# A retention layer and a token/channel mixer on one core: the state recurrence as one scan, the first token mixing inside the channel sums, wide q rows, and a scheduler that simulates its DMA queues

## The chip, the core and the metric

The kernel runs on one core of a Trainium2 chip. Times are device microseconds (us) of that core. The engines are called TensorE (PE, matmul; PEld is its weight load), VectorE (DVE), ScalarE (ACT), GpSimd (POOL) and SyncE (SP). Each takes its own instructions in the order in which the program holds them; semaphores make one wait for another. Sixteen DMA engines move the data, fed by queues: q1 is fed by SP, q0 by POOL, q10 by ACT.

## The reference

The first stage is a retention recurrence over q, k and v of shape (4 batches, 8 heads, 768 tokens, 64). The second is a mixer: over the tokens, then over the channels, each with a relu and a residual sum.

```
gamma = 1 - 2 ** (-5 - arange(8));  scale = 1 / sqrt(64)
for t in range(768):
    state = gamma * state + outer(k[t], v[t])          # 64 x 64 for each batch and head
    y[t]  = scale * q[t] @ state
x  = y as (4, 768, 512)                                # heads side by side
u  = x + (relu(x.T @ w_tok1) @ w_tok2).T               # w_tok1 768 x 256, w_tok2 256 x 768
out = u + relu(u @ w_ch1) @ w_ch2                      # w_ch1 512 x 1536, w_ch2 1536 x 512
```

Everything is float32 at the outside; the matmuls take float16.

## The kernel before, in words

The tokens of a batch are split into six chunks of 128, the heads into four pairs of two (128 channels). The unit of the front is one pair p of one batch b, written (b,p); the unit of the back is half a batch, 384 tokens.

The front of a pair (`front`, L338) does this:
- `load` (L313) has brought k and q as float32 through SP's queue (tiles kf and qf, L325 and L322) and v as float16 through POOL's (L333). k is scaled by gamma to the power of minus the place in the chunk (L376 on ACT, L378 on DVE), q is only cast (L384, L386).
- k and q are turned so that the channels lie on the partitions: in batches 0 and 1 by TensorE transposes (L412) and a copy out of PSUM (L423), in batches 2 and 3 by transposing DMAs on SP's queue (L403).
- ST (L439): ten matmuls give the sum of k times v of each of the first five chunks, for both heads. A DVE copy (L448) and four instructions (L451) carry the state from chunk to chunk: U[c] = U[c-1] * gamma^128 + ST[c]. Two scalings (L462 or L464) write it as float16 into r16.
- QK (L482): twelve matmuls give the k-by-q products within the chunks; four DVE products with a triangular mask (L490) give am. Y (L504, L507) adds state times q and am times v. X (L520, L524) scales Y by the decay of the token and is kept as float32; L537 casts it (x16).
- T1 (L548, twelve matmuls) and a relu (L556) give h1 of the token mixing. In batches 1 to 3 T2 (L599, two groups of six) applies w_tok2, L607 adds it to X, L615 casts u, and u is turned into uT by transposes (L636, L642) or by a DMA (L626). In batch 0 uT comes straight from TensorE: G (L570, L573) sums w_tok2 times h1 and the transposed x in PSUM, L580 copies it out. There T2 and L607 are done as well, later, because X has to hold u for the last sum.

The back of a batch (`back`, L651) does, for each half: C1 (L668), 12 groups of four 384-wide matmuls with a relu each (L682), then C2 (L695), three groups of twelve 512-wide matmuls, each followed by a sum with X on DVE (L703) and a store through ACT's queue (L709).

The order of the work is not written by hand. Each step is an `Op` with the engines it may run on, costs, the ops it needs, and the buffers (`Slot`) that it takes. `arrange` (L123) places them one after the other by estimated start and priority; `wires` (L81) then estimates how long each DMA takes, and the two alternate for eight turns, of which the best is kept. Two lines hold weights back:

```
    for key, o in (("t1", casts_of[0, 2][0]), (("c1", 0), casts_of[0, 3][-1])):
        wops[key].deps.append(o)
```

so the request for w_tok1 comes after the q cast of (0,2), and that for the first third of w_ch1 after the last q cast of (0,3). All later requests on POOL's queue follow in order: w_tok2, the thirds of w_ch1 and w_ch2, v of batch 1 and so on. At the end, matmuls on a zero tile (L756) are put before TensorE work that starts after a planned gap in the first 30 us.

Of the kernel before, what the change touches and what calls it, by code (L numbers as in the profile page):

```python
# [10 lines left out]
FP = mybir.dt.float32  # L11
F16 = mybir.dt.float16
AF = mybir.ActivationFunctionType
ALU = mybir.AluOpType


@with_exitstack
def kernel(
# [13 lines left out]
    P = 128  # L32
# [17 lines left out]

    BUFS = dict(kf=4, qf=4, k16=3, q16=3, v16=6, kT=4, qT=4, U=2, r16=3, am=8, X=3, x16=5, h1=5, u16=3,
                uT=3, h2=2, o=4)
    BANKS = dict(first=range(0, 7), front=range(0, 5), back=range(5, 8), fill=range(7, 8))
    SEM = 80
    XB = 2
    ops = []

    class Slot:


        def __init__(self, tag):
            self.tag, self.users, self.tile, self.bank = tag, [], None, None

    class Op:


        def __init__(self, prio, ways, deps=(), takes=(), uses=(), guard=0, dma=None, after=(), behind=None):
            self.prio, self.ways = prio, ways
            self.deps = [d for d in deps if d is not None]
            self.after = [d for d in after if d is not None]  # L70
            self.takes, self.guard, self.dma, self.behind = list(takes), guard, dma, behind
            self.end = self.eng = self.lat = None
            for s in list(takes) + list(uses):
                s.users.append(self)
            ops.append(self)

    GEN = dict(SP=20, ACT=20)
    FIRST = dict(SP=600, POOL=1300, ACT=600)
    LAND = dict(SP=800, POOL=1000, ACT=1500)

    def wires(order):  # L81

        line = {"SP": [], "POOL": [], "ACT": []}
        for o in order:
            if o.dma:
                line[o.eng].append(o)
        at = {k: 0 for k in line}
        left = {k: 0.0 for k in line}
        made = {k: 0.0 for k in line}
        ready = {}  # L90
        for k, ops_ in line.items():
            g = 0.0
            for o in ops_:
                g = max(o.start + FIRST[k], g)
                ready[o] = g
                g += o.dma[0] * GEN.get(k, 8)
                o.made = g
        t, dt, n = 0.0, 40.0, sum(len(v) for v in line.values())
        while n:
            on = []  # L100
            for k, v in line.items():
                if at[k] < len(v):
                    o = v[at[k]]
                    if left[k] == 0:
                        if ready[o] <= t:
                            left[k] = float(o.dma[0])
                        else:
                            continue
                    on.append((k, o))
            round_ = sum(o.dma[1] for k, o in on)  # L110
            for k, o in on:
                step = dt / round_
                if o.made > t:
                    step = min(step, dt / GEN.get(k, 8))
                left[k] -= step
                if left[k] <= 0:
                    left[k] = 0
                    at[k] += 1
                    n -= 1
                    o.lat = 0.5 * (o.lat or t + LAND[k] - o.start) + 0.5 * (t + LAND[k] - o.start)  # L120
            t += dt

    def arrange():  # L123
        free = dict(PE=0, ACT=2500, DVE=0, POOL=400, SP=700)
        gens = [0, 0, 0]
        taken = {t: [] for t in BUFS}
        bank_of = {i: None for i in range(8)}
        todo, order = list(ops), []
        for op in ops:
            op.end = op.eng = None  # L130
            for s in op.takes:
                s.bank = None

        def freed(slot):
            if slot is None:
                return 0
            if any(u.end is None for u in slot.users):
                return None
            return max(u.end for u in slot.users) + SEM

        while todo:
            best = []
            for op in todo:
                if any(d.end is None for d in op.deps) or any(d.end is None for d in op.after):
                    continue
                if op.behind is not None and op.behind.end is None:
                    continue
                base, banks, ok = 0, [], True
                for d in op.after:
                    base = max(base, d.end)  # L150
                for s in op.takes:
                    if s.tag in BANKS:
                        got = [(t, i) for i in BANKS[s.tag] if i not in [x[1] for x in banks]
                               for t in [freed(bank_of[i])] if t is not None]
                        if not got:
                            ok = False
                            break
                        banks.append(min(got))
                        base = max(base, banks[-1][0])
                    else:  # L160
                        q_ = taken[s.tag]
                        n = len(q_) - BUFS[s.tag]
                        n += sum(1 for s2 in op.takes[:op.takes.index(s)] if s2.tag == s.tag)
                        if n >= 0:
                            t = freed(q_[n])
                            if t is None:
                                ok = False
                                break
                            base = max(base, t)
                if not ok:  # L170
                    continue
                pick = None
                for w in op.ways:
                    start = max(base, free[w[0]])
                    for d in op.deps:
                        if d.eng == w[0] and (d.dma or d.eng == "PE"):
                            continue
                        start = max(start, d.end + (30 if d.eng == w[0] else SEM) + op.guard)
                    done = start + w[2] + (300 if w[0] == "DVE" else 0)
                    if pick is None or done < pick[0]:  # L180
                        pick = (done, start, w)
                best.append((pick[1], op, pick[2], banks))
            t = min(b[0] for b in best)
            eng = min(best, key=lambda b: (b[0], b[1].prio))[2][0]
            start, op, way, banks = min((b for b in best if b[2][0] == eng and b[0] <= t + 20),
                                        key=lambda b: b[1].prio)
            free[eng] = start + way[1]
            op.start, op.eng, op.emit = start, eng, way[3]
            if op.dma:
                op.end = start + (op.lat or 2200 + op.dma[0] * op.dma[1])  # L190
                if eng == "SP":
                    free["SP"] = max(start + 550, gens[-2])
                    gens.append(max(start + 550, gens[-1]) + op.dma[0] * GEN["SP"])
            else:
                op.end = start + way[2]
            banks = list(banks)
            for s in op.takes:
                if s.tag in BANKS:
                    s.bank = banks.pop(0)[1]
                    bank_of[s.bank] = s  # L200
                else:
                    taken[s.tag].append(s)
            todo.remove(op)
            order.append(op)
        return order
# [8 lines left out]
    def act(n, scaled=False):  # L214
        t = 186 + (93 if scaled else 0) + 5 * n // 6
        return t - 60, t + 20

    def dve(n, per=1.04):
        return int(140 + n * per), int(170 + n * per)

    def pool(n):
        return int(150 + n * 0.9), int(230 + n * 0.9)

    def one(eng, cost, emit):
        return [(eng, cost[0], cost[1], emit)]

    def either(emit, **costs):
        return [(e, c[0], c[1], lambda emit=emit, e=e: emit(e)) for e, c in costs.items()]


    itp = const_p.tile([P, 1], FP, name="itp")
    lgs = const_p.tile([P, H], FP, name="lgs")
    lnsc = const_p.tile([P, 1], FP, name="lnsc")
    gk = const_p.tile([P, H], FP, name="gk")
    gy = const_p.tile([P, H], FP, name="gy")
    gp = const_p.tile([P, NP], FP, name="gp")
# [8 lines left out]
    def prep(eng, cost, emit, deps=(), prio=(0, -1)):  # L245
        return Op(prio, [(eng, cost, cost + 40, emit)], deps)
# [91 lines left out]
    def front(b, p):  # L338
# [252 lines left out]
        for hf in range(2):  # L591
# [10 lines left out]
            if not first:  # L602
                t2_done[b * NP + p] = t2
# [185 lines left out]
```

## Time and profile before

| what | value |
|---|---|
| time, median of 3 runs | 217.68 us (217.49 to 218.25) |
| span of the profiled execution | 215.9 us |
| mean granted TensorE clock | 0.976 |
| TensorE busy | 199.0 us |
| ACT, DVE, POOL busy | 113.1, 103.7, 55.9 us |
| DMA bytes, mean rate | 30.99 MB, 144 GB/s |
| share of 16 DMA engines, q1 / q0 / q10 | 50.8% / 35.6% / 8.3% |
| last matmul ends, last store's sum starts | 212.26 us |

The profile is that of one execution. Its span is the time from the first to the last instruction; the run's time holds 1.75 us more, taken against the median. A group in the profile is one source line on one engine: its busy time, how often it ran, its mean duration. The mean durations of matmuls overlap with their neighbours; the chain (what released what, followed back from the last instruction) gives the time that each adds. "SPq", "ACTq" and "POOLq" are an engine's issues of DMAs.

### The profile page before, as it was taken

The numbers are of one execution on the slowest core, as the hardware profiler recorded it, in microseconds if no ns is written. First come the engines' busy times: TensorE is split into PE (matmuls) and PEld (weight loads), VectorE is DVE, ScalarE is ACT, GpSimd is POOL, SyncE is SP. The second block draws the span as 40 slices with busy tenths as digits, with TensorE's granted clock in tenths as the row PEclk, the third lists the DMA queues.
The fourth block names the chain that finished last, engine by engine and source line by source line (L and its number), as shares of the span: only waits on it lengthen the run. The fifth ranks groups of instructions, "written<-read, shape, count | busy, mean of one in ns | idle before, by whom it ended". The sixth has DMA issues, their size and how long they took to land.

```text
span 215.9 us, 4706 instructions
## 1 busy us (share of the span) xinstructions
PE 199.0 (92%) x1893; PEld 123.0 (57%) x1893; DVE 103.7 (48%) x269; ACT 113.1 (52%) x244; POOL 55.9 (26%) x90
## 2 busy tenths in 40 slices
PE   7698799996999999859998699999999999999993
PEld 3465588552367765426665576676645645545541
DVE  6288947402579986118788368874012012012021
ACT  4468996772088964248361677542721712703700
POOL 8225862211016545004332134343000000000000
PEclk9969999999699999999999699999999999999999
DMA  7999999999999999999999998254202112012012
GB/s 156 197 179 263 221 211 219 200 203 181 188 185 226 169 136 162 243 259 173 163 216 159 207 158 165 49 85 108 66 5 105 38 45 101 3 49 99 0 52 99
DMA packets 93207, 30.99 MB, mean 144 GB/s; under 512 B 81920, under 2 KB 90112, under 8 KB 93184
## 3 DMA queue, kind: packets, MB, share of 16 engines
q1 hardware_dynamic: 60672, 17.31, 50.8%
q0 software_dynamic: 29056, 7.08, 35.6%
q10 hardware_dynamic: 3456, 6.29, 8.3%
q8 instruction: 15, 0.25, 0.5%
q14 instruction: 8, 0.07, 0.1%
HBM read 26.74 MB, written 6.29 MB: 153 GB/s over the span
## 4 chain that ended last, share of the span: by engine, by line
PE 69%; DMA 18%; SPq 5%; ACT 3%; DVE 2%; issue 1%; ACTq 0%; POOL 0%
PE bank L695 27%; PE bank L668 25%; DMA v<-in_v_dram 11%; DMA kf<-in_k_dram 5%; PE bank L599 4%; PE bank L548 4%; SPq L322 3%; PE bank L507 2%; PE bank L482 2%; DMA qf<-in_q_dram 2%; PE bank L504 2%; PE bank L439 2%; SPq L325 1%; ACT X L520 1%; DVE am L490 1%; PE bank L412 1%
## 5 line engine op out<-in xcount | busy, mean ns | idle before, releaser
L668 PE MATMUL bank<-uT,wc 128*128 128x384 f16 x384 | 69.4, 327 | 5.0 <-ACT h L682 5.0
L682 ACT ACTIVATE h<-bank 128x384 f16<-128x384 f32 x96 | 46.1, 491 | 49.9 <-DVE o L703 24.0
L695 PE MATMUL bank<-wc,h 128*128 128x512 f16 x288 | 69.3, 386 | 0.1
L668 PEld LDWEIGHTS <-wc 128*128 128x128 f16 x384 | 35.7, 98 | 27.9 <-issue 5.8
L703 DVE TENSOR_TENSOR o<-X,bank 128x512 f32<-128x512 f32 x24 | 16.5, 688 | 62.0 <-PE bank L695 61.9
L695 PEld LDWEIGHTS <-h 128*128 128x128 f16 x288 | 26.9, 99 | 29.1 <-issue 2.0
L490 DVE TENSOR_TENSOR am<-bank,mask 128x384 f16<-128x384 f32 x64 | 32.1, 550 | 21.4 <-PE bank L482 21.3
L333 POOL DMA_DIRECT2D v<-in_v_dram x16 | 16.7, 1043 | 20.9 <-PE bank L507 10.9
L520 ACT ACTIVATE X<-bank,gy 128x192 f32<-128x192 f32 x50 | 18.0, 419 | 7.1 <-PE bank L507 6.9
L537 POOL CAST x<-X 128x384 f16<-128x384 f32 x23 | 12.0, 521 | 30.2 <-ACT X L520 16.4
L607 DVE TENSOR_TENSOR X<-X,bank 128x384 f32<-128x384 f32 x32 | 16.3, 550 | 5.8 <-PE bank L599 5.4
L615 POOL CAST u<-X 128x384 f16<-128x384 f32 x23 | 11.3, 509 | 28.7 <-DVE X L607 25.6
L451 DVE SCALAR_TENSOR_TENSOR U<-U,gp,bank 128x64 f32<-128x64 f32 x64 | 17.8, 278 | 1.5
L507 PE MATMUL bank<-v,am 128*128 128x64 f16 x192 | 15.0, 197 | 0.5 <-DVE am L490 0.4
L376 ACT ACTIVATE k<-kf,gk 128x384 f16<-128x384 f32 x22 | 12.8, 609 | 3.4 <-DMA kf<-in_k_dram 3.3
L599 PE MATMUL bank<-h,wt 128*128 128x128 f16 x192 | 14.0, 225 | 0.7 <-ACT h L556 0.7
L507 PEld LDWEIGHTS <-am 128*128 128x128 f16 x192 | 12.9, 101 | 2.8 <-DVE am L490 0.8
L462 ACT ACTIVATE r<-U 64x320 f16<-64x320 f32 x26 | 12.1, 467 | 3.5 <-DVE U L451 3.1
L599 PEld LDWEIGHTS <-wt 128*128 128x128 f16 x192 | 12.2, 101 | 2.8 <-issue 0.9
L386 POOL CAST q<-qf 128x768 f16<-128x768 f32 (+1 forms) x12 | 9.8, 815 | 15.2 <-DMA qf<-in_q_dram 15.2
L756 PE MATMUL bank<-zero 128*128 128x384 f16 x53 | 12.5, 382 | 1.2 <-DVE zero L248 1.2
L548 PE MATMUL bank<-x,wt 128*128 128x128 f16 x192 | 13.4, 219 | 0.2 <-DMA wt<-in_moe_w_tok_dram 0.2
(56 smaller groups left out, 154.0 us busy)
## 6 DMA issues: line engine op xcount, KB each, us to landing
kf<-in_k_dram SPq DMA_DIRECT2D x16, 384.0 KB, 9.3
qf<-in_q_dram SPq DMA_DIRECT2D x16, 384.0 KB, 9.8
out_dram<-o ACTq DMA_DIRECT2D x24, 256.0 KB, 2.0
v<-in_v_dram POOLq DMA_DIRECT2D x16, 192.0 KB, 14.6
wc<-in_moe_w_ch_dram POOLq DMA_DIRECT2D x6, 512.0 KB, 16.5
wt<-in_moe_w_tok_dram POOLq DMA_DIRECT2D x2, 384.0 KB, 7.6
kT<-k SPq DMA_TRANSPOSE x8, 6.1
qT<-q SPq DMA_TRANSPOSE x8, 6.2
```

Of the source, the lines that this page charges most:

```text
L333: nc.gpsimd.dma_start(out=tile_of(s, [P, 2, NC, D], F16), in_=v[b, 2 * p:2 * p + 2].rearrange("h (c p) d -> p (h c) d", p=P))
L451: nc.vector.scalar_tensor_tensor(U[:, c], U[:, c - 1], gp[:, p:p + 1], o, ALU.mult, ALU.add)
L490: nc.vector.tensor_tensor(am, src, m, ALU.mult)
L507: nc.tensor.matmul(o[:, j * D:(j + 1) * D], AM[2 * hf + j].tile[:, i], V.tile[:, j, c], start=(c == 0), stop=(c == 0 or j == 1))
L520: nc.scalar.mul(X.tile[:, half(hf), h * D:(h + 1) * D], yv[:, :, j * D:(j + 1) * D], gy[:, h:h + 1])
L548: nc.tensor.matmul(acc[:, jt * P:(jt + 1) * P], wt1[:, i, jt * P:(jt + 1) * P], X16.tile[:, i], start=(i == 0), stop=(i == NC - 1))
L599: nc.tensor.matmul(acc[:, i * P:(i + 1) * P], wt2[:, jt, t], H1.tile[:, jt], start=(jt == 0), stop=(jt == NJ - 1))
L607: nc.vector.tensor_tensor(xo, xo, T2.tile[:, :HC * P].rearrange("p (i d) -> p i d", d=P), ALU.add)
L668: nc.tensor.matmul(acc[:, :SH], w[:, ct, (ft % FW) * P:(ft % FW + 1) * P], UT.tile[:, ct, sh * SH:(sh + 1) * SH], start=(ct == 0), stop=(c ...
L682: nc.scalar.activation(H2.tile[:, ft], A.tile[:, :SH], AF.Relu)
L695: nc.tensor.matmul(A.tile, H2.tile[:, ft, i * P:(i + 1) * P], wc2[ft // FW][:, ft % FW], start=(ft == 0), stop=(ft == NF - 1))
L703: nc.vector.tensor_tensor(o, X.tile[:, sh * HC + i], A.tile, ALU.add)
```

## The change

- **Scan.** The copy and the four L451 become one `tensor_tensor_scan` over 320 elements, with the state's columns outside and the five chunks inside. Its factor tile `gsc` (128 x 4 x 320, zero at each first chunk so that the columns stay apart) is filled on DVE at the start. ST writes PSUM in the same order, with a stride of five elements. The r16 scalings go to ACT or POOL, no longer to DVE, and read U with that stride.
- **First token mixing.** In batch 0, T2 and L607 are left out. h1 of the four pairs is kept in one tile `h1_0`, and each C2 group of batch 0 begins with two 512-wide matmuls of w_tok2 with `h1_0`, so that the sum in PSUM already holds the mixing.
- **Wide q rows.** In batches 0 and 1, a partition takes six tokens in a row (1536 bytes) and no longer two runs of three (768 bytes). The copy of qT out of PSUM, which puts the tokens back in order, is two instructions for two halves. qf has three buffers for four.
- **Batch 0 of the back.** Both halves of C1 come before C2, on five PSUM banks; the first four groups of C1 take pairs 0 to 2 first and pair 3 apart.
- **Order.** The new `arrange` steps through time: each engine takes the first ready op by rank, and the three DMA queues (`Rings`) are stepped alongside, one descriptor of each queue in turn. It runs once. Costs are new (a transposing DMA holds SP for 1200 ns and not 100, for one). The two lines that held weights back are gone. Outside batch 0, QK of a pair is one op of twelve matmuls. In batch 0, X may also be written by DVE.

```diff
+        on = [(q, l[0]) for q, l in self.line.items() if l and l[0][2] <= t]
+            round_ = sum(x[0].dma[1] for _, x in on)
+            for q, x in on:
+                n = dt / round_
...
-    BUFS = dict(kf=4, qf=4, k16=3, q16=3, v16=6, kT=4, qT=4, U=2, r16=3, am=8, X=3, x16=5, h1=5, u16=3,
+    BUFS = dict(kf=4, qf=3, k16=3, q16=3, v16=6, kT=4, qT=4, U=2, r16=3, am=8, X=3, x16=5, h1=5, u16=3,
                 uT=3, h2=2, o=4)
-    BANKS = dict(first=range(0, 7), front=range(0, 5), back=range(5, 8), fill=range(7, 8))
+    BANKS = dict(first=range(0, 7), front=range(0, 5), back=range(5, 8), back0=range(3, 8))
...
+        nc.vector.memset(mask1, 1.0)
+        nc.vector.memset(gsc, 0.0)
+        for p in range(NP):
+            g = gsc[:, p].rearrange("p (e c) -> p e c", c=NC - 1)
+            nc.vector.memset(g[:D, :, 1:], g128[2 * p])
+            nc.vector.memset(g[D:, :, 1:], g128[2 * p + 1])
...
-                    nc.sync.dma_start(out=t.rearrange("p h (f i) d -> p h f (i d)", f=2),
-                                      in_=r.rearrange("h (f p i) d -> p h f (i d)", f=2, p=P))
+                    nc.sync.dma_start(out=t.rearrange("p h i d -> p h (i d)"),
+                                      in_=r.rearrange("h (p i) d -> p h (i d)", p=P))
...
-                    d = d.rearrange("d (f p i) -> d f p i", f=2, i=HC)[:, hs]
-                    o = o.rearrange("d (f i p) -> d f p i", f=2, i=HC)[:, hs]
+                    d = d.rearrange("d (f p i) -> d f p i", f=2, i=NC)[:, hs]
+                    o = o.rearrange("d (i f p) -> d f p i", f=2, i=NC)[:, hs]
+                    for f in range(d.shape[1]):
+                        (nc.scalar.copy if e == "ACT" else nc.vector.tensor_copy)(d[:, f], o[:, f])
...
-            st = tile_of(ST, [P, 512], FP)
+            st = tile_of(ST, [P, 512], FP)[:, :EC].rearrange("p (e c) -> p c e", c=NC - 1)
...
-        for c in range(NC - 1):
-            def emit(c=c):
-                o = ST.tile[:, c * D:(c + 1) * D]
-                if c == 0:
-                    U = tile_of(US, [P, NC - 1, D], FP)
-                    nc.vector.tensor_copy(U[:, 0], o)
-                else:
-                    U = US.tile
-                    nc.vector.scalar_tensor_tensor(U[:, c], U[:, c - 1], gp[:, p:p + 1], o,
-                                                   ALU.mult, ALU.add)
+            nc.vector.tensor_tensor_scan(out=tile_of(US, [P, EC], FP), data0=gsc[:, p], data1=ST.tile[:, :EC],
+                                         initial=0.0, op0=ALU.mult, op1=ALU.add)
...
-        r0 = op(either(lambda e, f=emit: f(e, 0), ACT=(400, 470), DVE=(460, 490)),
+        r0 = op(either(lambda e, f=emit: f(e, 0), ACT=(365, 470), POOL=(400, 470)),
...
+            return
         U16 = Slot("u16")
...
                         if f0 == 0:
                             tile_of(A, [P, 512], FP)
+                            if b == 0:
+                                for jt in range(NJ):
+                                    nc.tensor.matmul(A.tile, wt2[:, jt, t], h1_0[:, jt], start=(jt == 0), stop=False)
...
+        both = b == 0
...
+        if both:
+            widen(0)
+            widen(1)
+            narrow(0)
+            narrow(1)
...
-    for key, o in (("t1", casts_of[0, 2][0]), (("c1", 0), casts_of[0, 3][-1])):
-        wops[key].deps.append(o)
-    best = None
-    for turn in range(8):
-        order = arrange()
-        wires(order)
...
+    total, order, start, end = arrange(ops, BUFS, BANKS, rank)
```

What the change moves on the engines, read from the built programs: on TensorE, the transposes of q of (0,0) now come before those of k; Y of (0,2) and T1 of all pairs stand behind the transposes of (0,3); ST of (1,0) stands behind both halves of C1 of batch 0 and nine two-matmul steps of its C2. On POOL, the requests for w_tok1, w_tok2 and the first third of w_ch1 stand directly behind the four v requests of batch 0 and the mask; the other weights stand between casts, the last two behind the cast of q of (0,3). On ACT, the cast of q of (0,0) is the first instruction, and three q casts remain of five; POOL has thirteen instructions of that kind. On DVE, the factor tile is filled before the decay factors' exponents; the scaling of half of k of (1,0) stands ahead of the relu of T1 of (0,3). On ACT, the other half stands ahead of five of the eight uT copies of batch 0. On SP, each pair's loads in batches 2 and 3 alternate with the transposing DMAs. The zero matmuls are 52 for 53.

## The prediction, as put on record before the run

> **What bounds the kernel now.** I read the page's engine totals and slices first, then the chain in order of time, then the queue behind each gap that the chain shows.
>
> ```profile
> PE 199.0 (92%) x1893; PEld 123.0 (57%) x1893; DVE 103.7 (48%) x269; ACT 113.1 (52%) x244; POOL 55.9 (26%) x90
> PEclk9969999999699999999999699999999999999999
> DMA  7999999999999999999999998254202112012012
> ```
>
> TensorE is busy almost throughout, and the DMA engines are full until about 130 us. Single matmul rows overlap, so I price by the chain, which holds no overlap:
>
> ```profile
> 10.95 10.53 DMA kf<-in_k_dram
> ...
> 29.98 24.40 DMA v<-in_v_dram
> 54.42 0.35 PE bank L439 x10
> 54.77 4.38 PE bank L695 x12
> ...
> 88.81 4.52 DMA qf<-in_q_dram
> 93.41 0.35 ACTq L709
> ...
> 196.65 7.80 PE bank L668 x48
> 204.45 7.78 PE bank L695 x36
> 212.26 0.69 DVE o L703
> ```
>
> The end gives the prices: one 384-wide matmul of L668 is 7.80/48 = 0.1625 us, one 512-wide of L695 7.78/36 = 0.216. Other chain pieces give 0.056 for a 128-wide one (L599, L548, L412), 0.28 for the ten of L439 and 0.44 for the twelve of L482. Call the L668 group C1, L695 C2, L599 T2, L548 T1, L570 with L573 G, L482 QK, L504 with L507 Y, L439 ST, L412 TR; (b,p) is batch and pair. Work after C1 of batch 0 starts at 36.62: four batches of 96 x 0.1625 + 72 x 0.216 = 31.15, so 124.6; front of batch 1 16.1, of batches 2 and 3 12.1 each (no TR), less one TR done earlier: 164.5 us. TensorE ends at 212.26, so of 175.64 us about 11.1 are lost. They are:
> - 2.5 waiting for v of (1,0) until 54.42, then 1.8 at a slow clock (4.38 for twelve C2 that cost 2.59);
> - 3.3 from 91.0 to 94.35: ACT stood in a q cast for a qf that SP issued only at 88.81, and C1's relus were queued behind it;
> - 2.6 around 118 to 121 (ACT's output issue behind DVE), then about 1.2 at the slow clock.
>
> ```profile
> 83.78 4.95 SPq L403 DMA_TRANSPOSE kT<-k  x1
> 88.81 0.53 SPq L325 DMA_DIRECT2D qf<-in_q_dram  x1
> ```
>
> These rows of SP's timeline show why that qf was late: SP takes its issues in order, and the transposes ahead of it held it for 5 us each. Before 36.62 the last loads of batch 0 rule: k of (0,3) lands at 21.5, q of (0,3) at 22.8, and 11.2 us later (33.95) the last G is done; T2 of batch 0 (48 x 0.056 = 2.7) fills the rest.
>
> The span is 215.93; the run's time is 217.68 in the median, so 1.75 lie around the span. The end of TensorE plus 3.67 (last add and store) plus 1.75 is my time.
>
> **The change, part by part.**
>
> *Token mixing of batch 0.* 48 T2 matmuls go: -2.69. Twelve 512-wide ones come into C2: +2.59. Eight adds of 0.55 us leave DVE. On TensorE this is nothing; it moves 2.7 us from before C1 to after it.
>
> *Scan.* Per pair, a copy of 0.220 and four L451 of 0.278, 1.33 us, become one scan of 320 elements, which no row shows. One pass over 384 elements takes 0.550 (L490), so 0.47 scaled; at half that rate 0.94. I take 0.7, nearer neither: 16 x 0.63 = 10 us off DVE, which is 48% busy and not on the path, so 0 in the sum. It also removes five chances to interleave a mask; at worst 0.4 us in the last pair. [...] ST now writes PSUM at a stride of five elements, which no row shows: between 0 and a doubling of 16 x 0.28 = 4.5. ACT's permuted read of qT costs 803 ns against 799 for the straight kT, so I take 0.
>
> *Setup and small steps.* The scan's factor tile costs DVE about 3.3 us at the start (1280 elements at L725's 0.485 per 512, and eight smaller fills), so the decay factors, done at 4.1 now, come near 6; ACT also casts q of (0,0) first, and that q lands at 6.7. So the first k scale moves from 4.65 to about 7.7. Cover: ST of (0,0) waits for v until 9.97 and k of (0,1) lands at 10.2. Without it, up to 3 us. Two qT copies of 0.482 for one of 0.803: +0.16 on ACT, eight times, off the path. Eight r16 scalings go to POOL; the nearest row is its cast at 0.51, POOL is 26% busy: 0.
>
> *Weights no longer held back.* This is the largest term. Before, the first weight is requested at 19.3 and the six C1/C2 weights from 23.2, behind q casts on POOL; after, three requests follow the v's and a mask at some 6 to 9 us, the rest stand between casts. They move past the loads of pair (0,3). From the DMA packet records, per engine: k packets (256 B) alone go 52.6 per us, so a load of 96 takes 1.9 us. Beside C1/C2 weights (40 to 46 us) both go 9.4 per us: one for one, 106 ns a pair, so 10.2 us for the same load. A t1 weight packet alone takes 50 ns, a t2 packet 134, a v packet beside k 39 for both. Now, from 16 to 22 us, the queue of k and q has the engines to itself and moves 1.44 MB, 3.7 loads. That goes. At 16.0 the v's are nearly through (368 of 384) and k of (0,3) has yet to come. The wide q rows (16 packets per engine for 32; a 768-byte packet took 42 to 49 ns, so between 45 and 98; I take 75) bring the q loads through sooner, and leave some 40 v packets. Then k of (0,3): 40 x 39 + 48 x 70 + 8 x 152 ns = 6.2, packets through at 22.3; q of (0,3): 8 x 209 + 8 x 172 = 3.0, at 25.4. Landings came 1.7 after the mean packet before: 27.1 for q, against 22.8. TensorE's new order puts Y of (0,2) and all T1 behind the transposes of (0,3), so the whole 11.2 us tail shifts: last G at 38.3. Then k of (1,0) beside the weights: 10.2 more, landed at 37.3; its scaling stands on DVE ahead of the relu of (0,3), on ACT ahead of five uT copies: +1.0. **C1 starts at 39.3**, bounds 34.0 (q as now) to 43.4 (no v left beside them: from 17.5, k 48 x 70 + 16 x 152 + 32 x 106 ns = 9.2 and q 2.8 land at 31.2, + 11.2 + 1.0).
>
> *The order.* ST of (1,0) now stands behind both halves of C1 and nine steps of C2, some 23 us after C1's start; v lands before 54.4: the 4.3 at 54 go. New: q of (1,0) lands near 40, its transposes stand 1.3 us after C1's start: 0.5. Of the 7.1 later lost, the 3.3 need a q cast on ACT behind a late SP; three casts are left there for five, so it goes; of the 3.8, with DVE 10 us lighter, I keep 3.0. Bounds 0 and 11 (that all comes back with the TensorE order moved). While TensorE waits for pair (0,3), its clock may fall: the 2.5 us wait at 52 was followed by 3.4 us at half speed in the slices, the 3.3 at 91 by none. I take 0.7, bounds 0 and 3.4. [...]
>
> **Sum.** 39.3 + 164.5 + 2.6 + 0.5 + 0.7 + 3.0 = 210.6; + 3.67 + 1.75 = **216.0**.
>
> **Rivals.**
> 1. *The weights starve the start* (slower): the mechanism above at its far end. Every us that q of (0,3) is later costs one us, since TensorE is in order. For: the one-for-one rows. Against: a longer v phase shields k. It decides when C1 starts after 41.0 (39.3 + 1.7), q landing after 28.8. At 31.2 C1 starts at 43.4: 43.4 + 171.3 + 5.4 = 220.1.
> 2. *No harm at the start*: v's packets last through k of (0,3) and q lands as now. C1 at 34.5, 1.5 lost: 34.5 + 167.1 + 1.5 + 5.4 = 208.5; halfway, 211.
> 3. *Nothing*: TensorE's work is the same within 0.1 us and the gaps only move: 217.7.
>
> **Chances and range.** Forecast 0.44 (0.08 of it within 0.3%), rival 1 0.34, rival 2 0.18, rival 3 0.04. A difference under 0.3% can't be told from none here. So faster 0.54, same 0.12, slower 0.34. The range takes half of rival 2 and most of rival 1: 210.0 to 222.0; the forecast's own 214 to 218.
>
> **What would show it.** First C1 near 39 (mine), 34 (rival 2), 42 or later (rival 1); k of (0,3) scaled near 25 and not 21.5; no wait at ST of (1,0); L451's 17.8 us replaced by 8 to 15; the gaps of TensorE after 60 us summing to 3. It is wrong if q of (0,3) lands as now, or if a new queue-head wait on ACT, DVE or SP takes over 4 us later on.

## The result and the profile after

The changed kernel takes 211.58 us in the median of four runs (209.00 to 213.21), against 217.59 for the kernel before on the same chip. The ratio is 0.9651, with a 95% interval of 0.9581 to 0.9722: about 7.6 us faster. The two longer runs of the four (213.21 and 212.95) had a lower granted clock (0.984 and 0.980) and are left out of the ratio, as such runs are in every ratio below. The profiled execution took 210.22 us, its span is 208.5, the mean clock 0.988.

I predicted 216.0 with a range of 210 to 222. The direction was right and the size was not: the gain is over four times the 1.7 us forecast.

The page after, in the same three lines as before (engine totals, granted clock, DMA share):

```profile
PE 197.6 (95%) x1856; PEld 121.9 (58%) x1856; DVE 104.7 (50%) x218; ACT 103.3 (50%) x210; POOL 62.9 (30%) x100
PEclk9999969999999999999999999999999999999998
DMA  6999999999999999999999999972053012012012
```

TensorE is busy for 95% of the span and not 92, and its clock has one low slice (26 to 31 us) and not three. DVE's busy time did not fall, although the recurrence is cheaper: the factor tile (3.3 us), eighteen writings of X there for seven before (9.9 us for 3.9) and copies of kT (4.2 for 0.9) fill most of the place.

The chain of the changed kernel (start, duration, what):

```profile
2.58 21.59 DMA qf<-in_q_dram x2
...
24.97 0.52 PE bank L506 x6
...
26.05 0.88 PE bank L579 x12
...
36.33 1.30 PE bank L781 x8
...
59.54 0.40 PE bank L542 x10
...
204.83 0.69 DVE o L827
```

It has two parts. Until 24.2 us the loads of batch 0 rule; q of (0,3) is the last. From 24.97 on, the chain is TensorE almost alone. L781 (C1) starts at 36.33; L542 (ST) of (1,0) runs at 59.54 in its turn, where the kernel before waited for v until 54.42; TensorE ends at 204.83, for 212.26 before. The chain leaves TensorE for some us around 75 and 134, but TensorE had other work there.

To compare versions I cut the span at one point: the end of the last G of batch 0. It is at 33.77 before and at 35.99 after. From there to TensorE's end are 178.4 us before and 168.8 after. In the changed kernel TensorE's timeline shows one wait in that stretch, 0.49 at 139.25; I leave it in and take 168.8 as the work. The kernel before has T2 of batch 0 there (2.69) for the twelve matmuls folded into C2 (2.59), and the ten matmuls of ST cost 0.28 there for 0.40, in twelve pairs: its work is 168.8 + 0.1 - 12 x 0.12 = 167.5, and **10.9 us were lost**. So the change lost 2.2 us at the start and won 9.6 behind it. What has to be explained is why the waits went, and why the start paid so little.

### The profile page after: what moved, and what is told of

Same layout as the page of the kernel before. It is cut to its first block, busy times and chain, and to the rows that moved or that the text cites. A ratio compares the mean times of both kernels' runs of the same rounds, so it can differ in the third digit from the quotient of the medians.

```text
span 208.5 us, 4578 instructions
## 1 busy us (share of the span) xinstructions
PE 197.6 (95%) x1856; PEld 121.9 (58%) x1856; DVE 104.7 (50%) x218; ACT 103.3 (50%) x210; POOL 62.9 (30%) x100
## 3 DMA queue, kind: packets, MB, share of 16 engines
q0 software_dynamic: 29056, 7.08, 34.5%
## 4 chain that ended last, share of the span: by engine, by line
PE 81%; DMA 10%; DVE 3%; ACT 1%; POOL 1%; SPq 1%; issue 1%; DVEq 0%; POOLq 0%; ACTq 0%
PE bank L781 29%; PE bank L818 29%; DMA qf<-in_q_dram 10%; PE bank L651 5%; PE bank L712 3%; PE bank L579 3%; PE bank L542 2%; PE bank L610 2%; PE bank L607 2%; PE bank L506 2%; PE bank L681 1%; PE bank L816 1%; DVE am L593 1%; POOL r L560 1%; DVE U L547 1%; ACT r L558 1%
## 5 line engine op out<-in xcount | busy, mean ns | idle before, releaser
L781 PE MATMUL bank<-uT,wc 128*128 128x384 f16 x384 | 67.7, 326 | 0.0
L781 PEld LDWEIGHTS <-wc 128*128 128x128 f16 x384 | 35.9, 98 | 22.9
L558 ACT ACTIVATE r<-U 64x320 f16<-64x320 f32 x24 | 18.8, 782 | 10.7 <-DVE U L547 10.3
L640 POOL CAST x<-X 128x384 f16<-128x384 f32 x26 | 13.3, 512 | 32.9 <-DVE X L627 21.9
L719 DVE TENSOR_TENSOR X<-X,bank 128x384 f32<-128x384 f32 x24 | 12.2, 549 | 12.1 <-PE bank L712 12.0
L482 POOL CAST q<-qf 128x768 f16<-128x768 f32 (+1 forms) x13 | 10.6, 812 | 21.8 <-DMA qf<-in_q_dram 21.8
L727 POOL CAST u<-X 128x384 f16<-128x384 f32 x21 | 10.2, 508 | 22.6 <-DVE X L719 22.6
L623 ACT ACTIVATE X<-bank,gy 128x192 f32<-128x192 f32 x28 | 10.2, 416 | 10.3 <-PE bank L610 10.2
L547 DVE TENSOR_TENSOR_SCAN U<-gsc,bank 128x320 f32<-128x320 f32 x16 | 13.0, 814 | 1.8 <-PE bank L542 1.4
L627 DVE TENSOR_TENSOR X<-bank,gyw 128x384 f32<-128x384 f32 x18 | 9.9, 552 | 6.5 <-PE bank L610 6.4
L607 PE MATMUL bank<-r,qT 128*128 128x128 f16 x80 | 12.7, 222 | 0.1
```

The costliest lines, as they stand in the source:

```text
L547: nc.vector.tensor_tensor_scan(out=tile_of(US, [P, EC], FP), data0=gsc[:, p], data1=ST.tile[:, :EC], initial=0.0, op0=ALU.mult, op1=ALU.add)
L558: nc.scalar.mul(RS.tile[r, :, r], u, g128[2 * p + j])
L607: nc.tensor.matmul(o, QT.tile[:, c * P:(c + 1) * P], R[:, c - 1], start=True, stop=False)
L640: (nc.vector if e == "DVE" else nc.gpsimd).tensor_copy(X16.tile[:, half(hf)], X.tile[:, half(hf), pc])
L781: nc.tensor.matmul(acc[:, :SH], w[:, ct, (ft % FW) * P:(ft % FW + 1) * P], UT.tile[:, ct, sh * SH:(sh + 1) * SH], start=(ct == 0), stop=(c ...
```

## The experiments

The last three columns of this table are from profiled executions, in us; "lost" is the stretch from the last G to TensorE's end, less the work of that version reckoned as above. Times are medians of all runs; the ratio is to the kernel before on the same chip. One execution stands behind each of these three columns: the kernel before and its four variants with no change in time (b_sp1200, b_lane, b_lanectl, b_lane2) spread from 33.3 to 36.6 in the last G and from 7.6 to 11.8 in what is lost, so a difference of 2 or 3 us between two "lost" values tells little.

| run | what it is | time, median | ratio [95%] | last G | G to end | lost |
|---|---|---|---|---|---|---|
| before | | 217.68 | | 33.8 | 178.4 | 10.9 |
| after | | 211.58 | 0.965 [0.958, 0.972] | 36.0 | 168.8 | 0 |
| e_oldplan | new work, old planner | 211.66 | 0.980 [0.973, 0.987] | 33.6 | 172.6 | 3.8 |
| e_oldwork | old work, new planner | 221.27 | 1.019 [1.011, 1.026] | 46.0 | 170.3 | 2.8 |
| e_oldwork_hold | the same, weights held back | 210.55 | 0.972 [0.968, 0.976] | 34.8 | 170.4 | 2.9 |
| e_narrow | after, q rows of 768 bytes | 219.23 | 1.009 [1.005, 1.013] | 46.3 | 168.8 | 0 |
| e_narrowhold | the same, weights held back | 209.06 | 0.965 [0.960, 0.970] | 33.9 | 170.4 | 1.6 |
| e_hold | after, weights held back | 209.57 | 0.969 [0.963, 0.974] | 34.6 | 169.5 | 0.7 |
| e_holdc1 | after, w_ch1 alone held back | 209.87 | 0.971 [0.964, 0.978] | 37.2 | 169.5 | 0.7 |
| e_noscan | after, recurrence in four steps | 210.87 | 0.974 [0.967, 0.980] | 36.5 | 169.4 | 2.0 |
| e_sp100 | after, SP cheap in the plan | 211.30 | 0.968 [0.959, 0.977] | 34.0 | 168.8 | 0 |
| e_indep | e_oldwork_hold, queues planned apart | 245.41 | 1.126 [1.118, 1.134] | 58.2 | 181.6 | 14.1 |
| b_scan | before + scan | 215.76 | 0.994 [0.989, 0.998] | 35.0 | 175.4 | 6.5 |
| b_fold | before + T2 in C2 | 215.53 | 0.994 [0.991, 0.998] | 35.2 | 175.7 | 8.3 |
| b_both | before + both halves of C1 first | 216.24 | 0.995 [0.992, 0.999] | 33.9 | 177.5 | 10.0 |
| b_sp1200 | before + true SP cost in its planner | 216.75 | 0.999 [0.996, 1.003] | 35.3 | 175.6 | 8.1 |
| b_lane | before + a small DMA on SP | 217.43 | 1.002 [0.998, 1.006] | 34.0 | 176.1 | 8.6 |
| b_lanectl | the same, later | 217.74 | 1.002 [0.997, 1.006] | 33.3 | 179.3 | 11.8 |
| b_lane2 | the same, on ACT | 216.88 | 0.997 [0.993, 1.000] | 36.6 | 175.1 | 7.6 |

**Work and order apart.** The first pair crosses the two halves of the change. e_oldplan does all the new work in the order of the old planner:

```diff
-    total, order, start, end = arrange(ops, BUFS, BANKS, rank)
+    for turn in range(8):
+        order = arrange_old()
+        wires(order)
```

> All the new work (scan, mixing inside C2, wide q rows, both halves of C1 first), but placed by the planner of before (its DMA estimate, eight turns). Theory O, that the new order closes TensorE's gaps after C1 begins: 214 to 219 us, with over 5 us lost again after C1's start. Rival W, that the lighter steps (scan, eight adds fewer) close them whatever the order: 208 to 212 us, under 2 us lost.

e_oldwork puts the old work into the new scheduler, without the two lines that held weights back: the recurrence in four steps, T2 and L607 in batch 0, narrow q rows and four qf, batch 0 of the back by halves. (h1 of batch 0 stays in its own tile.)

```diff
-    BUFS = dict(kf=4, qf=3, ...
+    BUFS = dict(kf=4, qf=4, ...
-        both = b == 0
+        both = False
...
```

> The work of before (four-step recurrence, T2 and add in batch 0, q rows of 768 bytes, C1 and C2 half by half, four qf buffers), placed by the new planner, no weights held back. Theory O: 208 to 212 us, under 2 us lost after C1's start. Rival W: 214 to 219 us.

e_oldplan gave 211.66 with 3.8 lost, e_oldwork 221.27 with 2.8 lost. So each half by itself closes most of the waits, and the second is nevertheless slower than before, since its last G ends at 46. How the new work does so under the old planner was taken apart no further than by the single parts below. With so late a start the loads of batch 1 could have got ahead, and the 2.8 have been a gift of the delay. e_oldwork_hold takes that away:

```diff
+    for key, o in (("t1", casts_of[0, 2][0]), (("c1", 0), casts_of[0, 3][-1])):
+        wops[key].deps.append(o)
```

> The work of the kernel before (recurrence in four steps, T2 and its sum in batch 0, narrow q rows, batch 0 of the back by halves) in the order of the new scheduler, with the two weights held back as before. Theory O (the order alone closes the waits after the start): last G at 34 to 36, C1 start 36 to 38 and TensorE ends 169 to 171 us after the last G, time 210 to 213: almost the whole gain without any of the new work. Rival D (the same order without holding lost little after the start only because it started 10 us late and the loads had got ahead; the waits come back with a start on time): TensorE ends 174 to 178 us after the last G, time 214 to 218. Where it lies between, both have a share.

With the start back at 34.8 the lost time stays at 2.9, and the time is 210.55. **The order alone, with almost none of the new work, brings about four fifths of the gain** (2.8% of 3.5%; the intervals overlap). "Order" is here the whole new scheduler, with its costs, its ranks and its queues. In the changed kernel the wait at 91 is gone although the q load of (2,3), which SP issued at 88.81 before, is issued even later. Its timeline, the load and then the cast of it:

```profile
92.03 0.58 SPq L421 DMA_DIRECT2D qf<-in_q_dram  x1
...
102.12 0.83 POOL L482 CAST q<-qf 128x768 f16<-128x768 f32 x1
```

e_oldwork_hold issues it at 89.98 and casts at 100.78. In the kernel before, the cast of that q ran on POOL at 100.58, 7 us after the load had landed. So the load was not late for the work that needs it in any of these three orders; before, something else stood waiting for it. What that was is taken up below.

**The start.** e_narrow keeps the order of the changed kernel and gives the q rows back their 768 bytes:

```diff
-                    nc.sync.dma_start(out=t.rearrange("p h i d -> p h (i d)"),
-                                      in_=r.rearrange("h (p i) d -> p h (i d)", p=P))
+                    nc.sync.dma_start(out=t.rearrange("p h (f i) d -> p h f (i d)", f=2),
+                                      in_=r.rearrange("h (f p i) d -> p h f (i d)", f=2, p=P))
```

> The new kernel in its very order, only q of batches 0 and 1 again in rows of 768 bytes (and qT copied in one instruction). Theory N, that narrow rows together with weights requested early starve k and q of (0,3), as in the run with the old work under the new planner: last G of batch 0 near 44 to 47 us instead of 36.0, time 217 to 221. Rival, that the bad start there came from the other edits (buffers, order): last G 36 to 38, time 209 to 212.

It took 219.23: k of (0,3) is scaled and q of (0,3) is cast about 9 us later than in the changed kernel (21.18 and 24.30 there). Timeline of e_narrow:

```profile
29.73 0.62 ACT L471 ACTIVATE k<-kf,gk 128x384 f16<-128x384 f32 x1 [4.60 <-DMA kf<-in_k_dram]
...
33.77 0.62 POOL L482 CAST q<-qf 128x384 f16<-128x384 f32 x1 [9.21 <-DMA qf<-in_q_dram]
```

e_narrowhold has the narrow rows and holds the weights back.

> The changed kernel with q rows of 768 bytes again and the two weights held back again as before (order planned anew). Theory of the interplay: narrow rows alone cost 10 us at the start only because the early weights share the DMA engines with k and q of pair (0,3); with the weights held back the narrow rows are harmless: last G of batch 0 at 34 to 36 us, TensorE 169 to 171 us more, time 209 to 212. Rival, that narrow rows cost the start by themselves: last G at 40 or later, time 216 to 219.

```profile
23.09 0.51 POOL L482 CAST q<-qf 128x384 f16<-128x384 f32 x1
```

The same cast of q of (0,3) stands at 23.09 and waits for nothing, and the time is 209.06. So narrow rows cost nothing by themselves, and early weights cost little with wide rows; the two together cost about 10 us. That was the prediction's first rival, and the wide rows are what keeps it off. The DMA records of the traces show how, in packets per engine: in the changed kernel, k of (0,3) moved beside 94 packets of v and 20 of w_tok1; in e_narrow only 5 packets of v were left when it began, and it moved beside 108 of the three weights.

e_hold and e_holdc1 hold weights back in the changed kernel itself, both or w_ch1 alone:

```diff
+    wops["c1", 0].deps.append(casts_of[0, 3][-1])
```

> The new kernel with the two lines that hold the first weights back (w_tok1 after the q cast of (0,2), w_ch1 after the last q cast of (0,3)); the plan is made anew with them. If early weights delay the last k and q of batch 0, as the prediction had it: q of (0,3) lands near 22.8 and not 24.2, C1 starts 1 to 2 us earlier than 36.3, and the time is 208 to 210. Rival: T1, C1 and v of (1,0) now wait for weights that come later, C1 starts no earlier, and the time is 211 to 215.

> The changed kernel with only the first third of w_ch1 held back until the last q cast of (0,3); w_tok1 and w_tok2 are still asked for early. Theory of the interplay: T1's weights are there early and the big weights no longer share with k of (0,3), so last G at 33.5 to 35, and nothing is lost behind: time 207.5 to 209.5, the best of all versions. Rival (the weights early are harmless with wide rows, as the start of the changed kernel shows, and holding c1 moves the wait to C1): last G at 35.5 to 36.5 or C1 waits for its weight, time 209.5 to 212.

e_hold gains 1.4 at the start and gives half back behind it (209.57). In e_holdc1 the last G came at 37.2 and not at 34. There k of (0,3) was scaled only at 24.4 (21.2 in the changed kernel): it moved beside 66 packets of v and 42 of w_tok1 and w_tok2. That execution was the slowest of the four (212.01, the others 209.14 to 210.28), so its start need not be the usual one. None of these is separated from the changed kernel by its interval; no version tried is clearly better than it.

**The scan.** e_noscan keeps the order and does the recurrence in four steps again, with no stride in PSUM:

```diff
-            nc.vector.tensor_tensor_scan(out=tile_of(US, [P, EC], FP), data0=gsc[:, p], data1=ST.tile[:, :EC],
-                                         initial=0.0, op0=ALU.mult, op1=ALU.add)
+                    nc.vector.scalar_tensor_tensor(U[:, c * D:(c + 1) * D], U[:, (c - 1) * D:c * D], gp[:, p:p + 1], o,
+                                                   ALU.mult, ALU.add)
```

> The new kernel in its very order, but each scan is again one copy and four steps on DVE, ST writes PSUM without a stride and the r16 scalings read without one; the factor tile is gone. Theory O: 208 to 210.5 us, no slower: DVE's 13.0 us of scans become 21, ST goes from 0.40 back to 0.28 us for ten (1.9 us off TensorE), r16 on ACT from 782 to about 470 ns. Rival W: 212 us or more, because DVE becomes late for r16 and the masks.

210.87, and 0.6 us more from the last G to the end; the intervals of the ratios (0.967 to 0.980, and 0.958 to 0.972) do not separate it from the changed kernel. The scan frees DVE of 0.5 us per pair, and 2.0 us are lost without it, some of them in waits for U and r16 (0.75 at 74.0 the longest); but it costs elsewhere. Groups of the changed kernel (busy us, mean ns), and then of e_noscan:

```profile
L558 ACT ACTIVATE r<-U 64x320 f16<-64x320 f32 x24 | 18.8, 782 | 10.7 <-DVE U L547 10.3
...
L547 DVE TENSOR_TENSOR_SCAN U<-gsc,bank 128x320 f32<-128x320 f32 x16 | 13.0, 814 | 1.8 <-PE bank L542 1.4
```

```profile
L562 ACT ACTIVATE r<-U 64x320 f16<-64x320 f32 x24 | 11.2, 468 | 19.2 <-DVE U L551 18.9
```

One scan takes 0.81 us; scaling its strided result takes ACT 782 ns for 468; and ST, writing with the stride, takes 0.40 in the chain for 0.28 in e_noscan's.

**Single parts in the kernel before.** b_scan, b_fold and b_both each put one part into the kernel before; its own planner ordered them:

```diff
+        if b == 0:
+            widen(0)
+            widen(1)
+            narrow(0)
+            narrow(1)
```

> The kernel before with one edit: the four-step recurrence becomes one scan (factor tile, strided ST, r16 on ACT or POOL). Theory W, that a lighter DVE closes the later gaps (7.1 us at 91 and 118): 211 to 215 us. Rival, that the scan is neutral and ST's stride costs 1.9 us of TensorE: 217 to 219.5.

> The kernel before with one edit: T2 and its adds in batch 0 are left out, and C2 of batch 0 sums w_tok2 with h1. Theory, that TensorE's work is the same and only its place moves: C1 starts about 2.7 us earlier, 216 to 218.5 us. Rival, that the earlier C1 and eight adds fewer on DVE count: 213 to 215.

> The kernel before with one edit: in batch 0, both halves of C1 come before C2; its own planner makes the order. Theory, that the 4.3 us at 54 are lost only because ST of (1,0) stands too early: 212 to 214 us. Rival, that the planner moves ST along and TensorE waits for v as before: 216 to 218.

Each is worth 0.5 to 0.7%, at the edge of what can be told. In b_both the wait for v of (1,0) stayed, since the planner moved that ST along with the rest. TensorE in its timeline:

```profile
54.08 0.35 PE L439 MATMUL bank<-v,k 128*64 128x64 f16 x10 [1.54 <-DMA v<-in_v_dram]
```

**What in the scheduler.** The prediction laid the wait at 91 to SP, which transposing DMAs held ahead of the load. If that were a fault of the plan, its cost for these DMAs would matter. e_sp100 puts the 100 ns of the old op's line into the new scheduler. The old planner itself reserved 550 ns for any DMA on SP, whatever that line says; b_sp1200 raises this to 1200 (the shortest such DMA in the trace of before held SP for 1209 ns, the longest for 5420):

```diff
-                o = Op(ops, (0, b, p, 0), [("SP", 1200, 1200, emit)], dep, [dst], [src], dma=(48, 24))
+                o = Op(ops, (0, b, p, 0), [("SP", 100, 100, emit)], dep, [dst], [src], dma=(48, 24))
```

```diff
-                        free["SP"] = max(start + 550, gens[-2])
+                        free["SP"] = max(start + (1200 if op.dma == (48, 24) else 550), gens[-2])
```

> The changed kernel with a transposing DMA costed 100 ns on SP in the plan and not 1200, as the kernel before had it; the work is the same. Theory S (SP's true cost is what let the scheduler issue loads of q in time): the late q load behind transposes comes back, TensorE ends 171 to 174 us after the last G for 168.8, time 212 to 216. Rival (the simulated queues and the one-way order in time did it, SP's cost is a detail): 168 to 170, time 209 to 211.5.

> The kernel before, unchanged but for one cost in its own planner: a transposing DMA holds SP for 1200 ns there and not for 550. This is the prediction's reason for the 3.3 us lost at 91 taken alone. Theory S (the plan's wrong SP cost made that q load late): the wait at 91 goes or shrinks, TensorE ends 174 to 176 us after the last G (178.4 before), time 213 to 215.5. Rival (that planner places by estimates and then corrects, and one truer cost only moves the wait): 177 to 180, time 216 to 219.

e_sp100 lost nothing after the last G (168.8; this execution, 208.21, was the fastest of its four), and its ratio is that of the changed kernel. b_sp1200 cannot be told from the kernel before, and its timeline has the same load and ACT waiting for it:

```profile
89.00 0.54 SPq L325 DMA_DIRECT2D qf<-in_q_dram  x1
...
94.29 1.25 ACT L682 ACTIVATE h<-bank 128x384 f16<-128x384 f32 x3 [5.44 <-DMA qf<-in_q_dram]
```

So a truer cost is neither needed nor enough.

**What stood on ACT at 91.** In the built program of before there is no q cast on ACT between 48 and 107 us. The instruction ahead of the waiting relus is a store (the chain shown with the prediction has it: ACTq L709 at 93.41, directly behind the q load). The relus and TensorE behind them, in the timeline of before:

```profile
93.81 1.88 ACT L682 ACTIVATE h<-bank 128x384 f16<-128x384 f32 x4 [4.04 <-DMA qf<-in_q_dram]
...
94.35 1.78 PE L668 MATMUL bank<-uT,wc 128*128 128x384 f16 x10 [3.16 <-ACT h L682]
```

In the program as built, the DMAs of SP and ACT signal in turn on eight semaphores, and each is made to wait for the DMA eight places ahead of it on its own. In the trace of before, the 80 of them count on eight (101, 103 to 106, 116 to 118), ten on each, and of the 72 that have another ahead on theirs, 71 stand behind a wait on it. That store's eighth predecessor is the q load of (2,3), with which it has nothing else to do; in the trace both count on semaphore 116: the load is issued at 88.81, ACT's wait on 116 is over at 93.35, and the store goes out at 93.41. Three runs add one DMA of 256 bytes into an unused tile to the kernel before, so that the turns shift. b_lane has it on SP directly ahead of that q load, b_lanectl on SP behind the load (the store then shares with the load as before), b_lane2 on ACT:

```diff
+                if (tag, b, p) == ("qf", 2, 3):
+                    nc.sync.dma_start(out=extra, in_=k[0, 0, :1])
```

In b_lane2 this is nc.scalar; in b_lanectl it stands instead ahead of the store:

```diff
+                    count["o"] += 1
+                    if count["o"] == 6:
+                        nc.sync.dma_start(out=extra, in_=k[0, 0, :1])
```

> The kernel before with one DMA of 256 bytes into an unused tile more, on SP directly ahead of the q load of (2,3). The hardware DMAs of SP and ACT signal in turn on eight semaphores, and each waits for the DMA eight places earlier on its own; in the kernel before, the store of the last 128 tokens of batch 0 on ACT so waits for the q load of (2,3). With the extra DMA that store shares its semaphore with the small one, and nothing else is changed. Theory L (the wait at 91 is that store held by the shared semaphore, the relus of C1 behind it): no wait of ACT for a q load near 91, the 3.3 us go, TensorE ends 173.5 to 176 us after the last G for 178.4, time 212.5 to 215. Rival (the prediction's: a q cast on ACT waits there): the wait stays, 177 to 179, time 216 to 218.

> Control: the same extra DMA, but two DMAs ahead of the store, behind the q load of (2,3), and placed so that the store still shares its semaphore with that load. Theory L: the wait of ACT near 91 for the q load stays at 3 to 5 us, TensorE ends 177 to 179 us after the last G, time 216 to 218. Rival (any small shift of the queues removes the wait): as the first run.

The timeline of b_lane, the extra DMA and the relus of C1:

```profile
89.41 0.47 SPq L324 DMA_DIRECT2D extra<-in_k_dram  x1
...
92.89 1.88 ACT L686 ACTIVATE h<-bank 128x384 f16<-128x384 f32 x4 [2.90 <-DMA extra<-in_k_dram]
```

and of b_lanectl, the same relus:

```profile
94.24 1.88 ACT L684 ACTIVATE h<-bank 128x384 f16<-128x384 f32 x4 [3.94 <-DMA qf<-in_q_dram]
```

The wait took the name of the extra DMA, whose data nobody reads. Its only tie to ACT is the semaphore, so the mechanism is shown. Its price is not: the extra DMA came behind SP's transposes and was late itself, TensorE's wait there was 2.0 for 3.2, and the time did not move. In the control the store ahead was held as well, at 88.19 (its extra DMA comes only at 94.99), by the q load of (2,2) with which it shares: ACT's copy at 88.60 waited 4.29, and TensorE 2.46 and then 1.38. In the profiled execution of the kernel before, that store (86.42) shares with the same load, issued 9.5 us ahead of it, and was not held.

> The kernel before with the same extra DMA of 256 bytes, now issued by ACT at about 82 us; the store at 89 then shares its semaphore with the store at 82 and with no load. The run with the extra DMA on SP showed ACT's wait at 91 named after that extra DMA (2.9 us for 4.0). Theory L: ACT waits for no DMA between 88 and 95, TensorE's 3.3 us there go, it ends 173.5 to 176 us after the last G, time 1 to 3 us under the kernel before. Rival (another wait takes the place, since C1 there needs something else that is as late): 176.5 to 179, time as before.

In b_lane2 the store at 92.05 was free, but the store ahead of it now shared with a transpose that landed at 90.3, and ACT stood before that one:

```profile
90.78 0.80 ACT L646 COPY uT<-bank 128x768 f16<-128x768 f16 x1 [4.51 <-DMA qT<-q]
```

So the rival on the time held (0.997, interval 0.993 to 1.000): the stall went from one store to another. The changed kernel shares semaphores as well, but each of its stores was issued at least 8.5 us after the DMA with which it shares (4.6 us at 93.41 before), and ACT waits for no DMA there after 34 us. In e_oldwork_hold the least is 9.9 us. So these orders keep the partners apart, though nothing in the plan knows of the semaphores: that part of the gain was not designed. A kernel without any such sharing was not tried, and what the sharing costs in all stays open.

**The sharing of queues in the plan.** e_indep takes e_oldwork_hold and lets the scheduler step each DMA queue as if the others were idle:

```diff
-                n = dt / round_
+                n = dt / x[0].dma[1]
```

> The work of the kernel before in the order of the new scheduler, weights held back, as in the run that took 210.55 us, but the scheduler steps each DMA queue as if the other two were idle: it keeps its steps in time and its ranks and loses the sharing between queues. Theory Q (the simulated sharing is what makes the order fit the chip): waits come back, TensorE ends 173 to 178 us after the last G (170.4 with the sharing), time 213 to 218. Rival R (placing by rank as time goes on is what does it; the sharing is a detail): 169.5 to 172, time 209.5 to 212.

It took 245.41. The timeline shows why: loads land too early in the plan, so steps of batch 1 stand on ACT ahead of work of batch 0 (whose last G ends at 58.2), and the chip cannot bring their data in time.

```profile
40.03 1.12 ACT L469 ACTIVATE k<-kf,gk 128x384 f16<-128x384 f32 x2 [6.70 <-DMA kf<-in_k_dram]
...
44.08 0.83 ACT L478 CAST q<-qf 128x768 f16<-128x768 f32 x1 [2.93 <-DMA qf<-in_q_dram]
```

This order was only as good as the landing times that it was made with: 245.41 with the queues planned apart, 210.55 with them shared. In this scheduler the sharing of the queues is therefore needed. That it is the whole difference is not shown: the old planner also simulated shared queues, but only after placing, eight times in turn. Whether placing and stepping the queues in one pass is the cause, or the new ranks are, stays open.

## Why the prediction was wrong, step by step

The sum was 39.3 + 164.5 + 2.6 + 0.5 + 0.7 + 3.0 = 210.6 for TensorE's end, and 204.83 was measured. Three terms hold the difference: -3.0 at the start, -4.2 in the three loss terms, and +1.5 for the stride of ST: 210.6 - 3.0 - 4.2 + 1.5 = 204.9.

- **Start, wrong by 3.0.** The step that failed is "leave some 40 v packets" at 16 us. Fewer weight packets fell into the loads of (0,3): in the DMA records, 80 v packets per engine were left at 16 us, twice the 40 taken, v was still moving beside k of (0,3) until 20.6, and the first weight packets came at 17.4. Beside k stood 94 packets of v and 20 of w_tok1, for 40 of v, 48 of w_tok1 and 8 of w_tok2 in the sum; its packets were through at 20.6 for 22.3, those of q at 23.6 for 25.4. So k of (0,3) was scaled at 21.2 and not near 25, and q landed at 24.2 and not 27.1. Rival 2 (v shields the loads) described the start better than the forecast. Its far opposite, rival 1, is what e_narrow shows: q lands at 33.7 there, later than the 31.2 that I had priced. The price of a wide packet was right (75 ns taken, 78 measured).
- **The tail behind q**, taken as 11.2, was 11.8 (24.2 to 35.99). TensorE had waited 1.9 us for that q, and its granted clock was 0.50 from 26.02 to 29.44: QK took 0.88 for 0.44. This is what the clock term of 0.7 was for; it fell into this tail.
- **k of (1,0), +1.0, wrong.** It was scaled at 33.99 and not after 37.3, and its scaling ahead of the relu made TensorE wait nowhere.
- **Losses after the start, wrong by 4.2 (with the 0.7 and the 0.5).** The 2.5 at 54 and the 3.3 at 91 went, as forecast. "Of the 3.8 I keep 3.0" failed: of the waits a single one of 0.49 was left. I read DVE's load as the cause of the late waits and gave the new order no credit; e_oldwork_hold, with DVE busier than before (113.7 us for 103.7), closes 8.0 of the 10.9. Nor did the change make DVE lighter by 10 us: the scan saves 8.3, and in all DVE was busy 104.7 us for 103.7. The reading of the wait at 91, "ACT stood in a q cast", was wrong: it stood in a store that shares a semaphore with a q load. "Three casts are left there for five, so it goes" therefore came out true for a reason that has no part in it.
- **Stride of ST at 0, wrong.** 0.40 for 0.28 is 1.9 us in 16 pairs, 1.5 of them after the last G, inside the bounds of 0 and 4.5. I had carried over a permuted read by ACT to a strided write by TensorE, which no row showed.
- **Right:** the fold of T2 moved 2.6 us and cost nothing; the scan at 0.81 lies within the 0.47 and 0.94 that were estimated from L490's 0.550, nearer the second, and its place on the chain (74.23 and 136.01) held TensorE up by 0.5 at most. Rival 3 (nothing) fell.

## What to carry to other kernels

Price a new order by itself: waits came here from which step stood in front of which (TensorE's 3.2 us before 94.35 from one held store), so a schedule made with shared DMA queues can be worth as much as all the work saved under it, and gains of order and of work overlap (0.972 and 0.980 alone, 0.965 together). Where a wait names a load, look up which instruction waits: a store was held here until 93.41 by a load that it shares only a semaphore with. When two changes touch the same queue, such as early weights and wider rows, try them crossed: each alone looked harmless or useless, and together they decide 10 us. A small row of the chain for each memory layout (PSUM write, strided read) belongs in the sum before it is put at zero.

## What the runs showed of the hardware

- Ten matmuls of 64 columns that write PSUM at a stride of five floats took 0.40 us in the chain (after, L542), and 0.28 at stride one (e_noscan, L540).
- Reading float32 at that stride and writing float16 took ACT 782 ns (after, L558) for 468 (e_noscan, L562), and POOL 769 (L560) for 473 (L564), on 64 x 320.
- A store on ACT waited for a DMA of 256 bytes with which it shares nothing but a semaphore (b_lane): that DMA was issued at 89.41 beside other traffic, the store went out at 92.51, and the relus behind it had waited 2.9 us.
- The mean granted clock was 0.958 in e_narrow, where TensorE waited up to 4.6 us at a time between 18 and 34.5 us, and 0.930 in e_indep, with waits of up to 8.3; it was 1.000 in e_narrowhold and e_oldwork_hold, where TensorE never waited over 1.0 us at a time after 15 us.
- The length of one wait did not decide it. In the clock records of the two traces of before and after, the full stretches of half clock before TensorE's end are each 3.41 us long (from 11.22, 55.59 and 120.44 us before, from 26.02 after), and in before they begin whole multiples of 3.41 us apart. I divided both spans into windows of that length, laid from these starts. Of the 109 between 4 and 200 us at full clock, four were followed by half clock: they hold 1.17, 1.45, 1.50 and 1.53 us of matmuls. One with 1.47 was not, nor were the other 104, with 1.85 or more. In the kernel before, the wait until 54.42 left 1.17 us of matmuls in the window from 52.18, and half clock followed; the longer wait until 94.35 falls into two windows, with 1.47 and 2.20, and none followed. In the changed kernel 1.45 us from 22.61 on were followed by half clock from 26.02 to 29.44 (QK 0.88 for 0.44).
